# A late chunk's attention in one visit to the matrix engine: x in PSUM banks of its own, and a plan that counts loads and visits

## Chip, cores, metric

One core of one Trainium2 chip. The metric is device time in microseconds (us): the median of the runs shown, lower is better. A profile is one further execution, with every instruction of the engines recorded: PE (TensorE, matmuls), DVE (VectorE), ACT (ScalarE), POOL (GpSimd) and SP, whose queue issues the loads and part of the stores.

## What is computed

A linear attention with a decaying state, and then a two-layer network with a cosine gate on its output.

```python
# r, k, v: (4, 8, 768, 48); w, u: (8, 48)
for t in range(S):
    cur = np.einsum('bhd,bhe->bhde', u[None] * kt, vt)
    y[:, :, t] = np.einsum('bhd,bhde->bhe', rt, state + cur)
    state = w[None, :, :, None] * state + np.einsum('bhd,bhe->bhde', kt, vt)
x = y.transpose(0, 2, 1, 3).reshape(3072, 384)
h = x @ w_in                      # (384, 2048)
out = (h * np.cos(h)) @ w_out     # (2048, 384)
```

## The kernel before

**Attention in chunks.** The 3072 tokens are cut into 24 chunks of 128 tokens; chunk i is tokens of batch i % 4, and its predecessor in the recurrence is chunk i - 4. Within a chunk, the decay is put into k and r (`decT_k`, `decT_r`, `dec_k`), so that attention becomes matmuls: the scores A (k times r), the state update z (k times v), and the output x, which is a part from the state S and a part from v and the masked scores. The first 12 chunks (`EARLY`) go through `early()`, with transposes of k and r on PE (`tr`); the last 12 ("late") go through `in_halves()`: k and r are loaded in a layout that DVE transposes by itself, and the chunk is worked in two halves of 64 tokens. In all chunks POOL does three elementwise operations: r times k, the decay on k, and the product with u.

**The network in steps.** x of three chunks forms a block of 384 tokens; there are 8 blocks, and w_in and w_out are cut into 16 tiles f of 128. One step is one block with one f: on PE nine matmuls of 384 columns (here "H", line 302: 3 contraction tiles times the three products of a high and a low float part), then on ACT and DVE the chain qi, rest, cos, gate, gh, gl, then nine matmuls into the block's accumulator ("O", line 309, three for each chunk). There are 128 steps, so 1152 H and 1152 O matmuls. Blocks 0 to 3 go together through f 0-1, 2-4, 5-9, 10-15; blocks 4 to 7 one after the other. The weight tiles are loaded and converted ("conv": ACT, two DVE operations, POOL, ACT, DVE) while the first blocks run.

**PSUM.** Of the 8 banks, 0-2 hold the accumulators (`B_ACC`), 3-5 H's results (`B_H`), 6-7 the attention of late chunks (`B_ATT`): scores with z, and after them x, take turns in this pair. Early chunks' x use 6-7 or 4-5 (`B_EARLY`).

**Order.** Every piece of work is an operation (`op`) of a planner, with an engine, a due time, an assumed cost and buffers taken from rings. `one_pass` lists the operations in the order in which they can start, earliest due first; after each pass the due times are set to the latest possible starts, for `PASSES` passes; then all is emitted in that order. On each engine the order is fixed from then on. `CHUNK_DUE` and `TILE_SHIFT` are hand-set due times. Up to the first H, PE's planned gaps are filled with dummy matmuls (`warm_up`, one for each 0.2 us of gap).

A late chunk's PE work stands in three operations:

```python
last_A[0] = o_A = zo = op(PE, due - 1.7, 1.12, mm_az, [e_k, e_r, o_kd, l_v], [kT, rT, sp, kb, vb], lat=0.3)
x_1 = op(PE, due - 0.9, 1.1 if c else 0.9, mm_x, [e_r, l_v, e_A, o_s1], [rT, xp, vb, A, S1, *from_0], lat=0.3)
x_t = op(ACT, due - 0.8, 0.2, turn, [x_1], [xp])
xo = op(PE, due - 0.7, 0.6, lambda: from_v(1), [x_t], [xp, vb, A], lat=0.3)
```

`mm_az` is scores (line 1060) and z (line 1076); `mm_x` is x's first part, from the state and from v (line 1123); `from_v(1)` is its rest (line 1123 again), which has to come after a small ACT read, `turn`. Each stands where the planner puts it between H and O.

Of the kernel before, what the change touches and what calls it, by code (L numbers as in the profile page):

```python
# [39 lines left out]
CHUNK_DUE = (-17.2, -100.0, -17.0, -16.6, -14.0, -12.8, -11.2, -10.1, -1.3, 1.2, 13.7, 37.7)  # L40
TILE_SHIFT = (-9.7, 1.9, -82.4, -2.9, -12.4, 2.4, -14.7, 11.2, 1.4, 0.6, 6.8, 16.5)
PASSES = 6
# [20 lines left out]
class Op:  # L63
    def __init__(self, eng, due, cost, lat, emit, after, bufs, behind, port):
        self.eng, self.due, self.cost, self.lat, self.emit = eng, due, cost, lat, emit
        self.after = [o for o in after if o is not None]

        self.behind = behind

        self.port = port  # L70
        self.bufs = bufs
        self.end = None
        self.start = None
        for b in bufs:
            b.users.append(self)


class Plan:
# [9 lines left out]
    def op(self, eng, due, cost, emit, after=(), bufs=(), lat=0.2, line=None, port=False):  # L88

        o = Op(eng, due, cost, lat, emit, after, bufs, self.lines.get(line) if line else None, port)  # L90
# [81 lines left out]
    def one_pass(self):  # L172
# [19 lines left out]
        done, port = [], 0.0  # L192
        while len(done) < len(self.ops):
            best = None
            for eng, ops in cand.items():
                feas = []
                for o in ops:
                    r = self._ready(o)
                    if r is not None:
                        feas.append((max(free[eng], r[0], port if o.port else 0.0), o, r[1]))  # L200
# [3 lines left out]
                pick = min((f for f in feas if f[0] <= t0 + 0.01), key=lambda f: (f[1].due, f[1].seq))  # L204
# [8 lines left out]
            o.gap = t - free[o.eng]  # L213
            o.start, o.end = t, t + o.cost
            free[o.eng] = o.end
            if o.port:
                port = o.end
            cand[o.eng].remove(o)
# [9 lines left out]
def kernel(  # L228
# [47 lines left out]
    F_1 = CUTS[-2]  # L276
# [46 lines left out]
    with ExitStack() as actx:  # L323
# [11 lines left out]
        B_ATT = [pair(6)]  # L335
# [9 lines left out]
        r_all = att.tile([P, 2, H, DP], F32, name="r_all")  # L345
        R_r = [Tile(r_all[:, i]) for i in range(2)]
        raw_r = Tile(r_all.rearrange("q i h d -> q (i h d)")[:, 0 : 2 * DM].bitcast(I32).rearrange("q (f w) -> q f w", w=2))
# [10 lines left out]
        X_r = early_ring("r", 2, [P, H, DP])  # L358
# [10 lines left out]
        R_raw = ring("raw", 2, [P, DM, 2], I32) + [raw_r]  # L369
# [50 lines left out]
        def start_pads():  # L420
            for t in R_k + R_r + R_v + X_k + X_v + X_r:
# [36 lines left out]
        op(PE, -300, 1.6, start_banks, [o_dve], b_0)  # L458
# [22 lines left out]
        o_pow = op(DVE, -90, 3.5, powers, [o_wT, o_dve], [b_w, b_pow])  # L481
# [21 lines left out]
        def tab_copy():  # L503
# [9 lines left out]
            1.2,  # L513
            lambda: nc.sync.dma_start(u_b.rearrange("p h d -> p (h d)"), u.rearrange("h d -> (h d)").partition_broadcast(P)),
            lat=4.6,
# [988 lines left out]
```

## Time and profile before

| | |
|---|---|
| median of 3 runs | 514.6 us (514.23 to 518.33) |
| the profiled execution: its own time | 514.43 us |
| its span, first to last instruction | 512.7 us |
| mean granted TensorE clock | 0.995 |
| PE busy | 498.7 us (97%) |
| DVE, ACT, POOL busy | 383.6, 314.0, 177.3 us |

How to read it: matmuls are pipelined, so that a row's duration (0.34 us for a 384-column matmul) is longer than the distance to the next one (0.17 to 0.18 us); what counts on PE is the distance from start to start. A profile lists each attention matmul on fp32 tiles of an order's row twice (x16 in an order is x32 in the trace). Dummy matmuls count as busy.

### The profile page before, as it was taken

The numbers are of one execution on the slowest core, as the hardware profiler recorded it, in microseconds if no ns is written. First come the engines' busy times: TensorE is split into PE (matmuls) and PEld (weight loads), VectorE is DVE, ScalarE is ACT, GpSimd is POOL, SyncE is SP. The second block draws the span as 40 slices with busy tenths as digits, with TensorE's granted clock in tenths as the row PEclk, the third lists the DMA queues.
The fourth block names the chain that finished last, engine by engine and source line by source line (L and its number), as shares of the span: only waits on it lengthen the run. The fifth ranks groups of instructions, "written<-read, shape, count | busy, mean of one in ns | idle before, by whom it ended". The sixth has DMA issues, their size and how long they took to land.

```text
span 512.7 us, 14821 instructions
## 1 busy us (share of the span) xinstructions
PE 498.7 (97%) x5836; PEld 472.2 (92%) x5836; DVE 383.6 (75%) x788; ACT 314.0 (61%) x805; POOL 177.3 (35%) x183
## 2 busy tenths in 40 slices
PE   7999899999999999999999999999999999999994
PEld 5777789999999999999999999999999999999994
DVE  6888778889899996566777786767767777756452
ACT  1887676777776676547375665574663746654442
POOL 5876512246544463214426224133044042200000
PEclk9999899999999999999999999999999999999999
DMA  9978526577855875426484837448364475110001
GB/s 139 157 152 153 135 79 181 161 161 147 163 138 126 188 144 92 90 40 114 115 173 124 181 93 181 100 130 200 90 169 118 120 178 149 35 49 1 1 1 53
DMA packets 116657, 61.81 MB, mean 121 GB/s; under 512 B 80097, under 2 KB 112482, under 8 KB 116578
## 3 DMA queue, kind: packets, MB, share of 16 engines
q1 hardware_dynamic: 111250, 53.50, 43.0%
q0 software_dynamic: 5184, 7.08, 9.9%
q8 instruction: 47, 0.77, 0.7%
q14 instruction: 32, 0.26, 0.2%
q10 hardware_dynamic: 144, 0.20, 0.1%
HBM read 48.96 MB, written 11.80 MB: 118 GB/s over the span
## 4 chain that ended last, share of the span: by engine, by line
PE 88%; ACT 0%; issue 0%
PE psum L309 40%; PE psum L302 40%; PE psum L1123 4%; PE psum L1060 1%; PE psum L1076 1%; PE psum L989 1%; PE psum L958 0%; PE psum L978 0%; PE psum L1004 0%; PE psum L833 0%; ACT f L1320 0%; PE psum L605 0%
## 5 line engine op out<-in xcount | busy, mean ns | idle before, releaser
L309 PE MATMUL psum<-w_out_hi,gh 128*128 128x384 f32 x384 | 131.9, 344 | 0.0
L302 PE MATMUL psum<-xh,w_in_hi 128*128 128x384 f32 x384 | 131.5, 342 | 0.0
L309 PE MATMUL psum<-w_out_hi,gl 128*128 128x384 f32 x384 | 129.7, 338 | 0.0
L302 PE MATMUL psum<-xh,w_in_lo 128*128 128x384 f32 x384 | 129.7, 338 | 0.0
L309 PE MATMUL psum<-w_out_lo,gh 128*128 128x384 f32 x384 | 129.5, 337 | 0.0
L302 PE MATMUL psum<-xl,w_in_hi 128*128 128x384 f32 x384 | 129.4, 337 | 0.0
L314 ACT ACTIVATE qi<-psum 128x384 int32<-128x384 f32 (+1 forms) x132 | 62.9, 479 | 79.6 <-PE psum L302 78.8
L317 DVE SCALAR_TENSOR_TENSOR f<-psum,qi 128x384 f32<-128x384 f32 (+1 forms) x132 | 71.0, 540 | 47.4 <-ACT qi L314 46.6
L1293 DVE TENSOR_TENSOR gl<-f,gh 128x384 fp32r<-128x384 f32 (+1 forms) x132 | 83.9, 639 | 28.9 <-ACT gh L1290 28.0
L1290 ACT CAST gh<-f 128x384 fp32r<-128x384 f32 (+1 forms) x132 | 65.8, 501 | 40.0 <-DVE f L1287 20.0
L320 ACT ACTIVATE f<-f 128x384 f32<-128x384 f32 (+1 forms) x132 | 67.6, 514 | 30.9 <-DVE f L317 30.4
L1287 DVE TENSOR_TENSOR f<-psum,f 128x384 f32<-128x384 f32 (+1 forms) x132 | 70.6, 537 | 12.8 <-ACT f L320 10.9
L309 PEld LDWEIGHTS psum<-w_out_hi,gh 128*128 128x128 f32 x384 | 72.0, 187 | 2.4 <-issue 0.2
L302 PEld LDWEIGHTS psum<-xh,w_in_hi 128*128 128x128 f32 x384 | 72.5, 189 | 1.6 <-ACT T L942 0.2
L302 PEld LDWEIGHTS psum<-xl,w_in_hi 128*128 128x128 f32 x384 | 72.6, 189 | 0.0
L302 PEld LDWEIGHTS psum<-xh,w_in_lo 128*128 128x128 f32 x384 | 72.6, 189 | 0.0
L309 PEld LDWEIGHTS psum<-w_out_hi,gl 128*128 128x128 f32 x384 | 72.0, 188 | 0.0
L309 PEld LDWEIGHTS psum<-w_out_lo,gh 128*128 128x128 f32 x384 | 72.0, 187 | 0.0
L852 POOL TENSOR_TENSOR T<-T,decT_k 112x512 f32<-112x512 f32 x12 | 17.0, 1414 | 126.7 <-DVE T L847 50.8
L1335 POOL DMA_DIRECT2D out_dram<-f x36 | 33.3, 1080 | 41.0 <-ACT f L1320 40.6
L677 POOL TENSOR_TENSOR f<-f,raw 128x384 int32<-128x384 int32 x23 | 26.2, 1138 | 48.0 <-ACT gh L1290 15.7
L942 ACT ACTIVATE T<-ident,a 128x128 f32<-128x128 f32 x96 | 30.2, 391 | 1.2 <-DVE a L923 1.2
(124 smaller groups left out, 610.8 us busy)
## 6 DMA issues: line engine op xcount, KB each, us to landing
raw<-in_moe_w_out_dram SPq DMA_DIRECT2D x23, 384.0 KB, 3.6
out_dram<-f POOLq DMA_DIRECT2D x36, 192.0 KB, 5.0
raw<-in_moe_w_in_dram SPq DMA_DIRECT2D x72, 64.0 KB, 2.4
out_dram<-f SPq DMA_DIRECT2D x23, 192.0 KB, 2.0
r_all<-in_r_dram SPq DMA_DIRECT2D x40, 96.0 KB, 2.3
raw<-in_moe_w_in_dram SPq DMA_DIRECT2D x10, 384.0 KB, 4.0
raw<-in_k_dram SPq DMA_DIRECT2D x39, 96.0 KB, 2.2
v<-in_v_dram SPq DMA_DIRECT2D x18, 192.0 KB, 4.4
```

The lines of the kernel that those rows point to most:

```text
L302: nc.tensor.matmul(ph, a, b_, start=(i == 0), stop=(i == len(mm) - 1))
L309: nc.tensor.matmul(acc, a[:, ts], b_, start=(first and i == 0), stop=(last and i == 2))
L314: nc.scalar.activation(qi, ph, AF.Copy, scale=INV_2PI, bias=0.25)
L317: nc.vector.scalar_tensor_tensor(q, ph, INV_2PI, qi, op0=ALU.mult, op1=ALU.subtract)
L320: nc.scalar.activation(q, q, AF.Sin, scale=TWO_PI, bias=0.5 * math.pi)
L677: lambda: nc.gpsimd.tensor_tensor(ai(), ai(), cn(), op=ALU.add),
L942: nc.scalar.activation(A[j]()[:, p, :], ident, AF.Copy, scale=ab()[:, h : h + 1])
L1123: nc.tensor.matmul(xv()[G * g : G * g + G, kk, tokens(n)], lhsT, rhs, start=(kk // 2, g) not in opened, stop=True, skip_group_check=True,)
L1287: nc.vector.tensor_tensor(g()[:, cs], ph()[:, cs], q()[:, cs], op=ALU.mult)
L1290: nc.scalar.copy(gh()[:, cs], g()[:, cs])
L1293: nc.vector.tensor_tensor(gl()[:, cs], g()[:, cs], f32(gh())[:, cs], op=ALU.subtract)
L1335: nc.gpsimd.dma_start(dst, ob(), accum_op=ALU.add)
```

## The change

- **Visits.** PE operations carry `moe` (H and O: True; late attention: False) and a late chunk's operations a `visit` number. x's first part and rest of chunk i have visit i, the scores and z of chunk i + 1 have visit i too. When the last operation on an engine has a visit number and another one of that visit could start within `STAY`, the planner takes that one next. x's first part also waits for what the next chunk's scores and z need, and for its own state update.
- **Banks.** A late chunk's x moves from banks 6-7 to 4-5 (`B_X`), which are two of H's three banks; scores with z keep 6-7.
- **The planner's costs.** A change from H or O to late attention costs `SWITCH`; loads and stores have a transfer time (`dma`) on one shared resource, with a landing time worked out from it, and are not planned further than `DMA_AHEAD` ahead of it. Several PE and SP costs are set anew.
- **Due times.** Hand-set shifts for all 24 chunks and all 32 weight tiles in place of those for 12 and 12; 7 passes.
- **Buffers.** `r_all` with its third use as a raw weight buffer goes: early r has a ring of 4, raw weights a ring of 3, early chunks have two more T buffers; `w_out_1` holds 8 tiles in place of 10.
- **Dummies** may stand until the first O, no longer the first H.

```diff
+CHUNK_SHIFT = (
...
+TILE_SHIFT = (
...
+PASSES = 7
+SWITCH, STAY = 0.2, 0.3
+DMA_AHEAD, DMA_FIRST, DMA_LAST, DMA_LAND = 3.0, 1.3, 0.6, 1.95
...
-                        feas.append((max(free[eng], r[0], port if o.port else 0.0), o, r[1]))
+                        t = max(free[eng], r[0], port if o.port else 0.0, moved - DMA_AHEAD if o.dma else 0.0)
+                        feas.append((t, o, r[1]))
...
-                pick = min((f for f in feas if f[0] <= t0 + 0.01), key=lambda f: (f[1].due, f[1].seq))
+                last = on.get(eng)
+                stay = [
+                    f for f in feas if last and last.visit is not None and f[1].visit == last.visit and f[0] <= free[eng] + STAY
+                ]
+                if stay:
+                    pick = min(stay, key=lambda f: (f[0], f[1].due, f[1].seq))
+                else:
+                    pick = min((f for f in feas if f[0] <= t0 + 0.01), key=lambda f: (f[1].due, f[1].seq))
...
+            if o.moe is False and last and last.moe:
+                o.end += SWITCH
+            on[o.eng] = o
...
+            if o.dma:
+                moved = max(moved, t + DMA_FIRST) + o.dma
+                o.lat = max(moved + DMA_LAST - o.end, DMA_LAND)
...
-    F_1 = CUTS[-2]
+    F_1 = NF // 2
...
-        B_ATT = [pair(6)]
+        B_ATT, B_X = [pair(6)], [pair(4)]
...
-        X_r = early_ring("r", 2, [P, H, DP])
+        X_r, X_T = early_ring("r", 4, [P, H, DP]), early_ring("T", 2, [P, NP, C])
...
-        R_raw = ring("raw", 2, [P, DM, 2], I32) + [raw_r]
+        R_raw = ring("raw", 3, [P, DM, 2], I32)
...
-            bk = B_EARLY if i < EARLY else B_ATT
+            bk = B_EARLY if i < EARLY else B_X
...
-                A, sp, S1 = Buf(R_T), Buf(bk), Buf(R_s)
+                A, sp, S1 = Buf(R_T), Buf(B_ATT), Buf(R_s)
...
-                last_A[0] = o_A = zo = op(
-                    PE, due - 1.7, 1.12, mm_az, [e_k, e_r, o_kd, l_v], [kT, rT, sp, kb, vb], lat=0.3
-                )
+                ready = [e_k, e_r, o_kd, l_v]
+                last_A[0] = o_A = zo = op(PE, due - 1.7, 0.88, mm_az, ready, [kT, rT, sp, kb, vb], lat=0.3)
+                zo.visit, zo.moe = i - 1, False
+                if i - 1 in visits:
+                    visits[i - 1].after += ready
...
-                    1.1 if c else 0.9,
+                    0.99,
                     mm_x,
-                    [e_r, l_v, e_A, o_s1],
+                    [e_r, l_v, e_A, o_s1, *o_s2],
...
+                x_1.visit, x_1.moe = i, False
+                visits[i] = x_1
                 x_t = op(ACT, due - 0.8, 0.2, turn, [x_1], [xp])
-                xo = op(PE, due - 0.7, 0.6, lambda: from_v(1), [x_t], [xp, vb, A], lat=0.3)
+                xo = op(PE, due - 0.7, 0.27, lambda: from_v(1), [x_t], [xp, vb, A], lat=0.3)
+                xo.visit, xo.moe = i, False
...
             if i < EARLY:
-                due = CHUNK_DUE[i]
+                due = -1.5 * (EARLY - i) - 1.0
...
+            due += CHUNK_SHIFT[i]
...
-            if s == 0:
-                o_first = oh
+            oh.moe = True
...
+                oo.moe = True
+                if s == 0 and t == 0:
+                    o_first = oo
```

What this does to the order, at three places. In the rows a name's number is the buffer's; lines are those of each kernel, and H is line 302 before and 328 now, O 309 and 335, x 1123 and 1160, scores 1060 and 1093, z 1076 and 1109.

**PE, a late chunk.** Before, chunk 14's x with two O groups between its parts; its scores and z (buffers T_102, v_83) stand 36 rows ahead of it, alone, between an O and an H:

```order
L1123 MATMUL psum<-T_102,s_109 32x64 x16
L1123 MATMUL psum<-T_102,s_105 32x64 x16
L1123 MATMUL psum<-T_103,v_83 32x64 x16
L309 MATMUL psum<-w_out_hi_2188,gh_124 128x384
L309 MATMUL psum<-w_out_hi_2188,gl_126 128x384
L309 MATMUL psum<-w_out_lo_2189,gh_124 128x384
L309 MATMUL psum<-w_out_hi_2188,gh_124 128x384
L309 MATMUL psum<-w_out_hi_2188,gl_126 128x384
L309 MATMUL psum<-w_out_lo_2189,gh_124 128x384
L1123 MATMUL psum<-T_103,v_83 32x64 x16
```

Now, chunk 13's x with the scores and z of chunk 14 between its parts, an O before and after:

```order
L335 MATMUL psum<-w_out_lo_1918,gh_127 128x384
L1160 MATMUL psum<-T_105,s_111 32x64 x16
L1160 MATMUL psum<-T_105,s_108 32x64 x16
L1160 MATMUL psum<-T_106,v_81 32x64 x16
L1093 MATMUL psum<-T_107,T_101 64x64 x16
L1109 MATMUL psum<-v_82,k_79 48x48 x16
L1160 MATMUL psum<-T_106,v_81 32x64 x16
L335 MATMUL psum<-w_out_hi_1917,gh_127 128x384
```

Three visits have become one here. Over the whole order, late attention's groups between H or O number 36 before (three for each of 12 chunks) and 22 now: six are of this full form, two join a chunk's scores and z to the x of the chunk before, the rest stand as before.

**SP, the loads of early chunks 7 to 11.** Before, from the r of chunk 7 on, two loads of w_in tiles (raw_127, raw_128; the order of the loads is also that of the transfers) stand before the k of chunk 10:

```order
L763 DMA early_r_96<-in_r_dram 128x4x48 x2
L540 DMA raw_127<-in_moe_w_in_dram 32x2x256 x4
L540 DMA raw_127<-in_moe_w_in_dram 64x256 x2
L755 DMA early_v_94<-in_v_dram 128x8x48
L755 DMA v_81<-in_v_dram 128x8x48
L763 DMA k_80<-in_k_dram 128x4x48 x2
L763 DMA r_all<-in_r_dram 128x4x48 x2
L763 DMA early_k_89<-in_k_dram 128x4x48 x2
L763 DMA r_all<-in_r_dram 128x4x48 x2
L755 DMA v_82<-in_v_dram 128x8x48
L540 DMA raw_128<-in_moe_w_in_dram 32x2x256 x4
L540 DMA raw_128<-in_moe_w_in_dram 64x256 x2
```

Now, from the k of chunk 9 on, one w_in tile stands before the k of chunk 10 (early_k_89), and k and r of chunk 11 come before the next:

```order
L796 DMA early_k_88<-in_k_dram 128x4x48 x2
L796 DMA early_r_96<-in_r_dram 128x4x48 x2
L788 DMA v_82<-in_v_dram 128x8x48
L565 DMA raw_130<-in_moe_w_in_dram 32x2x256 x4
L565 DMA raw_130<-in_moe_w_in_dram 64x256 x2
L796 DMA early_k_89<-in_k_dram 128x4x48 x2
L796 DMA early_k_90<-in_k_dram 128x4x48 x2
L796 DMA early_r_97<-in_r_dram 128x4x48 x2
L788 DMA early_v_91<-in_v_dram 128x8x48
L565 DMA raw_131<-in_moe_w_in_dram 32x2x256 x4
L565 DMA raw_131<-in_moe_w_in_dram 64x256 x2
```

The second w_in tile has moved behind the last k and r, and the first from behind chunk 7's r to behind chunk 8's v.

**PE, the end of the early part.** Before, one H stands between chunks' transposes long before this place; here come chunk 8's z (line 1004), chunk 9's scores (958), chunk 11's transposes (833), chunk 10's scores, and two H in a row of which the first matmul is shown, with three chunks' x and z and chunk 11's scores still to come behind them:

```order
L1004 MATMUL psum<-v_83,k_80 48x48 x8
L958 MATMUL psum<-T_103,T_97 128x128 x8
L833 MATMUL psum<-ident,early_k_91 112x64 x8
L833 MATMUL psum<-ident,early_r_96 112x64 x8
L958 MATMUL psum<-T_99,T_101 128x128 x8
L302 MATMUL psum<-xh,w_in_hi 128x384
```

Now chunk 11's transposes (866) are followed by chunk 9's x (1011, 1022), chunk 10's scores (991), chunk 9's z (1037) and the very first H:

```order
L866 MATMUL psum<-ident,early_k_90 112x64 x8
L866 MATMUL psum<-ident,early_r_97 112x64 x8
L1011 MATMUL psum<-T_101,s_113 32x128 x16
L1022 MATMUL psum<-early_T_98,early_v_91 32x128 x4
L1022 MATMUL psum<-T_104,early_v_91 32x128 x4
L1022 MATMUL psum<-early_T_98,early_v_91 32x128 x4
L1022 MATMUL psum<-T_104,early_v_91 32x128 x4
L991 MATMUL psum<-T_102,T_103 128x128 x8
L1037 MATMUL psum<-early_v_91,early_k_88 48x48 x8
L328 MATMUL psum<-xh,w_in_hi 128x384
```

The H have moved behind the early chunks; behind the first H remain chunk 11's scores and two chunks' x and z. On POOL the three operations of all 12 chunks now stand before any weight tile's addition; before, two such additions stood among them.

More of the change, by code (lines that the diff above doesn't have):

```diff
@@ L63, with __init__ @@
 class Op:
-    def __init__(self, eng, due, cost, lat, emit, after, bufs, behind, port):
-        self.eng, self.due, self.cost, self.lat, self.emit = eng, due, cost, lat, emit
+    def __init__(self, eng, due, cost, lat, emit, after, bufs, behind, port, dma):
+        self.eng, self.due, self.cost, self.lat, self.emit = eng, round(due, 3), cost, lat, emit
+        self.dma = dma
         self.after = [o for o in after if o is not None]
@@ L70, in __init__ @@
         self.port = port
+        self.visit = None
+        self.moe = None
         self.bufs = bufs
@@ L86, in __init__, with op @@
         self.lines = {}
-    def op(self, eng, due, cost, emit, after=(), bufs=(), lat=0.2, line=None, port=False):
-        o = Op(eng, due, cost, lat, emit, after, bufs, self.lines.get(line) if line else None, port)
+    def op(self, eng, due, cost, emit, after=(), bufs=(), lat=0.2, line=None, port=False, dma=0.0, behind=None):
+        o = Op(eng, due, cost, lat, emit, after, bufs, self.lines.get(line) if line else behind, port, dma)
         if line:
@@ L213, in one_pass @@
             o.gap = t - free[o.eng]
+            last = on.get(o.eng)
             o.start, o.end = t, t + o.cost
+            if o.moe is False and last and last.moe:
+                o.end += SWITCH
+            on[o.eng] = o
             free[o.eng] = o.end
@@ L512 @@
             -23.9,
-            1.2,
+            0.5,
             lambda: nc.sync.dma_start(u_b.rearrange("p h d -> p (h d)"), u.rearrange("h d -> (h d)").partition_broadcast(P)),
-            lat=4.6,
+            lat=2.0,
+            dma=0.6,
+            behind=o_w,
         )
@@ L639, in cn @@
                 return raw()[:, :, 0]
-            o0 = op(SP, due - 3.5, 1.6 if part else 3.2, lambda: load_raw(i, raw, True), [behind], [raw], lat=3.4)
+            o0 = op(
+                SP,
+                due - 3.5,
+                0.5 if part else 3.8,
+                lambda: load_raw(i, raw, True),
+                [behind],
+                [raw],
+                dma=1.4 if part else 1.5,
+            )
             o2 = op(
@@ L718 @@
         last_A = [None]
-        early_done = []
-        r_first = Buf([raw_r])
+        early_done, visits = [], {}
         last_z = [None] * B
@@ L748, in chunk @@
             trp = Buf(B_TR)
-            kT, rT = Buf(R_T), Buf(R_T)
+            R_Tc = R_T + X_T if i < EARLY else R_T
+            kT, rT = Buf(R_Tc), Buf(R_Tc)
             xp = Buf(bk)
@@ L782, in chunk @@
                 ks, rs = Buf(R_raw), Buf(R_raw)
-            rbs = [rb] if late else [rb, r_first]
+            rbs = [rb]
             def load_r():
@@ L881, in chunk @@
                     due - 2.5,
-                    0.55,
+                    0.59,
                     tr,
-                    [l_r, l_k if first else o_kd, o_pool, o_pads],
+                    [l_r, l_k if first else o_kd, o_pool, o_pads, o_wT],
                     [*rbs, kb, trp, rT, kT],
@@ L934, in early @@
             def early():
-                A = [Buf(R_T) for _ in range(2)]
+                A = [Buf(R_Tc) for _ in range(2)]
                 Ap = [Buf(B_ONE) for _ in range(2)]
@@ L1339 @@
                         s + 2.5,
[L1340 removed]
+                        0.45 if f0 == 0 else 1.1,
                         st,
@@ L1343 @@
                         [ob],
-                        lat=2.5,
+                        dma=0.6 if f0 == 0 else 1.0,
                     )
```

42 lines of the change are left out of this document (22 added, 20 removed).

## The prediction

> **What bounds the kernel now.** First the page's busy times, then the busy time by stretches, then PE's rows.
>
> ```profile
> PE 498.7 (97%) x5836; PEld 472.2 (92%) x5836; DVE 383.6 (75%) x788; ACT 314.0 (61%) x805; POOL 177.3 (35%) x183
> ```
>
> 97% is an average that counts dummy matmuls. By stretches (length, then busy time and instructions of PE, PEld, DVE, ACT, POOL, granted clock, DMA share, GB/s):
>
> ```profile
> 20.00:25.00 5.00, 5.00 (x125) 4.25 (x125) 4.44 (x10) 4.93 (x16) 3.89 (x4) 1.00 0.89 161
> 55.00:60.00 5.00, 3.86 (x38) 3.64 (x39) 4.37 (x8) 4.47 (x14) 2.37 (x3) 0.73 0.65 169
> 83.00:219.00 136.00, 136.00 (x781) 136.00 (x780) 117.48 (x223) 93.38 (x210) 58.86 (x59) 1.00 0.65 143
> 219.00:481.00 262.00, 261.87 (x3530) 249.71 (x3529) 185.56 (x378) 150.68 (x403) 72.05 (x66) 1.00 0.47 115
> ```
>
> From 83 to 481 us PE is idle for 0.13 us of 398: there the time is the sum of what PE executes, and only fewer or denser matmuls help. Before that, as from 20 to 25 us, PE, DVE, ACT and POOL are all nearly full and the loads run at 161 GB/s; there the time is set by when the early chunks get through. The chain that ended last prices the network's work (start, length, matmuls):
>
> ```profile
> 58.05 4.56 PE psum L302 x18
> ...
> 93.17 1.56 PE psum L302 x9
> 94.73 1.58 PE psum L309 x9
> 99.45 3.12 PE psum L302 x18
> ```
>
> 128 steps of 1.56 + 1.58 make 402 us, and the change leaves them alone. So I sum two terms: what late attention costs PE, and what PE does outside H and O up to the end of early attention.
>
> **Term 1: visits.** PE's rows of chunk 12: scores and z, the O around x's first part, x's rest (start, time to the end of the row, what):
>
> ```profile
> 220.15 0.34 PE L309 MATMUL psum<-w_out_lo,gh 128*128 128x384 f32 x1
> 220.42 0.69 PE L1060 MATMUL psum<-T,T 48*64 48x64 f32 x32
> 220.93 0.54 PE L1076 MATMUL psum<-v,k 64*48 64x48 f32 x32
> 221.40 0.45 PE L309 MATMUL psum<-w_out_hi,gh 128*128 128x384 f32 x1
> 221.69 0.34 PE L309 MATMUL psum<-w_out_hi,gl 128*128 128x384 f32 x1
> ...
> 224.48 0.34 PE L309 MATMUL psum<-w_out_lo,gh 128*128 128x384 f32 x1
> ...
> 226.13 0.34 PE L309 MATMUL psum<-w_out_hi,gl 128*128 128x384 f32 x1
> ...
> 227.87 0.34 PE L302 MATMUL psum<-xh,w_in_lo 128*128 128x384 f32 x1
> 228.14 0.45 PE L1123 MATMUL psum<-T,v 64*32 64x64 f32 x32
> 228.52 0.44 PE L309 MATMUL psum<-w_out_hi,gh 128*128 128x384 f32 x1
> 228.81 0.33 PE L309 MATMUL psum<-w_out_hi,gl 128*128 128x384 f32 x1
> ```
>
> The pitch inside O is 1.58 / 9 = 0.176. From the last O to the first score it is 0.27, so entering costs 0.09 to 0.10; from the first O behind to the second 0.29, so leaving costs 0.11: about 0.205 a visit, and the rows around x's rest say the same. (From O's end to where the next O would have stood, the three visits displace 1.19, 1.30 and 0.59, together 3.08.) The order has 22 visits for 36: 14 joins. If a join cost nothing, 14 x 0.205 = **2.9 us** would go; that is one end. The other is that a join costs as much as leaving and entering: 0. No row shows x next to scores, but early attention has other tile shapes side by side in one visit:
>
> ```profile
> 71.05 0.34 PE L309 MATMUL psum<-w_out_lo,gh 128*128 128x384 f32 x1
> 71.32 1.16 PE L958 MATMUL psum<-T,T 48*128 48x128 f32 x16
> 72.41 0.67 PE L978 MATMUL psum<-T,s 48*32 48x128 f32 x32
> 73.01 1.08 PE L989 MATMUL psum<-T,early_v 128*32 128x128 f32 x32
> 74.02 0.44 PE L309 MATMUL psum<-w_out_hi,gh 128*128 128x384 f32 x1
> 74.30 0.34 PE L309 MATMUL psum<-w_out_hi,gl 128*128 128x384 f32 x1
> ```
>
> The last of 16 scores starts near 71.32 + 1.16 - 0.28 = 72.20 (0.28 is taken as one matmul's length), and x's first 0.21 later, against a pitch of 0.06 within the scores: 0.15 for the change of shape. In chunk 12, z's last starts near 220.93 + 0.54 - 0.21 = 221.26 (0.21 taken likewise) and O 0.14 later, against a pitch of 0.015: 0.12 of that sort is in the visit's own length already. A join so costs some 0.03 more than nothing: 14 x (0.205 - 0.03) = **2.4 us**, which I take, as the nearest rows have it.
>
> The Trainium skill, "TensorEngine Tiling (Array Packing)", section Key Properties, says that a change of tiling mode drains the engine. By it, a full visit still changes mode four times (in, x to scores, z to x, out) for six in three visits, and with a change at half of 0.205 the term would be some 1.4 (an estimate from that page's rule). The 0.15 above agrees that a change inside a visit is not free; the time by the rule, 508.9, lies in the forecast's band.
>
> What else the visits touch is priced at nothing, with this cover: x's ACT read and its copies run beside H and O; the added wait (x also waits for the next chunk's operands) has a whole chunk's distance, some 20 us, of loads ahead of it; behind a waiting x on PE stands everything, so a late one is paid in full.
>
> **Term 2: the early part.** Before, rows around the first H, chunk 11's transposes and chunk 9's z:
>
> ```profile
> 42.25 0.44 PE L302 MATMUL psum<-xh,w_in_hi 128*128 128x384 f32 x1
> ...
> 56.14 0.44 PE L833 MATMUL psum<-ident,early_k 64*112 64x64 f32 x8 [1.55 <-POOL early_k L874]
> 56.64 1.42 PE L958 MATMUL psum<-T,T 48*128 48x128 f32 x16
> 57.98 0.69 PE L302 MATMUL psum<-xh,w_in_hi 128*128 128x384 f32 x1
> ...
> 65.64 0.34 PE L302 MATMUL psum<-xh,w_in_lo 128*128 128x384 f32 x1
> 65.91 0.56 PE L1004 MATMUL psum<-early_v,early_k 128*48 128x48 f32 x16
> 66.41 0.44 PE L302 MATMUL psum<-xh,w_in_hi 128*128 128x384 f32 x1
> 66.69 0.34 PE L302 MATMUL psum<-xl,w_in_hi 128*128 128x384 f32 x1
> ```
>
> A visit of z displaces 66.69 - 65.64 - 2 x 0.174 = 0.70; scores with x 74.30 - 71.05 - 2 x 0.176 = 2.90; x alone 2.90 - 1.09 (71.32 to 72.41) = 1.81. Behind 57.98, early attention still needs 2.90 + 2 x 1.81 + 3 x 0.70 = 8.6, and the 18 H there take 4.56 for 3.12 at a clock of 0.73: 1.4 lost, of which 0.1 is the entry. One H (1.56) is done already. So H and O could start unbroken at 57.98 + 8.6 + 1.3 - 1.6 = **66.3**.
>
> In the new order the first H stands behind chunk 11's transposes (0.50, 56.14 to 56.64), chunk 9's x (1.61, 72.41 to 74.02), scores (1.09) and z (0.50): 3.7 in all. Behind it remain 2.90 + 1.81 + 2 x 0.70 = 6.1. What decides is when chunk 11's k is ready, which POOL's rows show:
>
> ```profile
> 11.89 1.09 POOL L864 TENSOR_TENSOR f<-early_r,k 128x384 f32<-128x384 f32 x1 [1.40 <-DMA early_r<-in_r_dram]
> ...
> 48.63 1.02 POOL L864 TENSOR_TENSOR f<-early_r,early_k 128x384 f32<-128x384 f32 x1 [3.47 <-DMA early_r<-in_r_dram]
> ...
> 55.07 1.01 POOL L874 TENSOR_TENSOR early_k<-early_k,dec_k 128x384 f32<-128x384 f32 x1
> ```
>
> At 11.89 it had waited for chunk 2's r, the 6th load of 192 KB, at 48.63 for chunk 10's r, the 34th when a w_in tile counts as two: 36.74 / 28 = 1.31 us each. In the new order chunk 10's k is the 33rd (one tile ahead of it in place of two) and lands at 11.89 + 27 x 1.31 = 47.3; chunk 11's r, the 35th, at 49.9. POOL then does five operations of 1.02 up to chunk 11's decayed k (product, decay, u for chunk 10; product, decay for chunk 11): 52.4. So PE's transposes start at 52.4, in place of 56.14, and the first H at 56.1. H and O could start unbroken at 56.1 + 6.1 = 62.2: a gain of **4.1 us**, which I take: between these loads stands a w_in tile, as between those of before. The other pace is the 161 GB/s of 20 to 25 us, 1.22 a load: k at 44.8, POOL done at 49.9. PE itself has some six and a half chunks of 3.7 to do after 25 us, to 49, and chunk 10's transposes and two z (1.5) stand ahead of chunk 11's, so 51 is its own bound: a first H at 54.7 and a gain of 5.5. The w_in tile's own conversion ends on POOL two operations after chunk 11's k (54.4), on ACT and DVE 1.1 later: 55.5, just in time. Weight tiles for O load later than before by one w_in tile, 2.6 us, and are needed 11.7 behind the first H (four H, two x, scores and z): hidden. The buffers' new rings and `w_out_1`'s size I price at nothing, since loads there start on the queue's turn, not on a buffer.
>
> **Sum.** 514.43 - 4.1 - 2.4 = 507.9 for the profiled execution; it stands 0.2 below the median of the runs, so **508.0**.
>
> **Rivals.**
>
> - *The clock drops again.* Chunk 10's decayed k is ready at 49.4 by the same count; with its transposes and two z PE is done at 51 and waits 1.4 for chunk 11's. Before, a wait of 1.55 stood ahead of the 0.73. Price 1.3, and a late w_in tile would add to it: 509.2 to 510.5. The page "TensorE: Matmul & The Clock Gate" of the Trainium skill, section "What's actually happening", has the clock fall after an idle window of about 3.4 us, so that such a wait alone would not do it; the trace, which had it after 1.55, disagrees, and the rival stays.
> - *Joins save nothing* (the visits do not do what they are for): 510.3.
> - *H runs out of banks.* x needs banks 4 and 5 at once, and until its copies are out, H has bank 3 alone. At the end of the kernel, a step's bank was free 2.3 us after H:
>
> ```profile
> 485.61 0.49 ACT L314 ACTIVATE qi<-psum 128x384 int32<-128x384 f32 x1 [0.31 <-PE psum L302]
> ...
> 487.29 0.56 DVE L1287 TENSOR_TENSOR f<-psum,f 128x384 f32<-128x384 f32 x1 [0.59 <-ACT f L320]
> ```
>
>   The gate ends at 487.85, qi began at 485.61. Between such a step's operations DVE also has late chunks' transposes:
>
> ```profile
> 248.97 1.09 DVE L847 STREAM_TRANSPOSE T<-r_all 128x512 f32<-128x512 f32 x1
> ```
>
>   In the new order most x have two or more groups between the youngest H but one and themselves, 3.7 us or more; the youngest has 2.1 if four O stand between. Where the youngest sits in bank 4 or 5, x waits 0.2 to 0.5: 12 x 0.3 = 3.6 and 511.5. It becomes **slower** if a DVE transpose of 1.09 stands ahead of the gate in each of the 12: 12 x (0.3 + 1.09) = 16.7, and 524.7; it decides from the point where the youngest H is closer than 2.3 us to x's banks. Against it: DVE is 71% busy there, and PE hardly waited in 398 us with the same chain.
> - *Loads at the fast pace*: 506.5.
>
> **How the numbers follow.** A measurement of this kernel tells about 1% (5.1 us) from no change: faster is below 509.4, slower above 519.7. Forecast, 506.8 to 509.4: 0.46. Fast loads or more, 504.5 to 506.8: 0.12. Clock or a late first H, 509.2 to 511: 0.16, a quarter of it below 509.4. Joins for nothing: 0.09. Banks, light: 0.12; banks, heavy: 0.05. Faster 0.46 + 0.12 + 0.04 = 0.62; slower 0.05; the same 0.33. The range, 504.5 to 512.5, leaves out the heavy case, part of the light one, and gains beyond both ends of the terms.
>
> **What the new profile would show.** Chunk 11's transposes near 52 and the first H near 56, with clock 1.00 from 55 to 60; H and O unbroken from about the point where 6 us of attention are behind the first H; 22 late visits, a full one displacing about 2.7 (3.08 for three before: 1.19, 1.30, 0.59) and a gap of some 0.15 between x and scores; no PE wait behind 83. Wrong would be: PE waiting for DVE's gate or x's copies in front of an x or an H (banks), a wait for POOL or a DMA at a visit (the added dependence), the first H behind 58 (loads), or full visits above 3.

## The result, and the profile after

The changed kernel takes 520.64 us (median of 17 runs, 517.28 to 522.43) against 514.57 for the kernel before on the same chip: 1.0107 times as long, 95% interval 1.0084 to 1.0130. It is slower by about 1.1%; forecast were 508.0 and a range of 504.5 to 512.5. The profiled execution took 521.12, with a span of 519.4.

The busy times by stretches, in the columns of the rows before (length, then busy time and instructions of PE, PEld, DVE, ACT, POOL, granted clock, DMA share, GB/s):

```profile
20.00:25.00 5.00, 5.00 (x128) 4.16 (x128) 4.62 (x10) 4.93 (x16) 4.67 (x6) 1.00 1.04 171
45.00:50.00 5.00, 3.19 (x31) 2.62 (x33) 4.16 (x9) 3.76 (x12) 3.32 (x4) 0.50 1.01 177
50.00:55.00 5.00, 5.00 (x74) 3.67 (x74) 3.24 (x6) 2.52 (x8) 2.60 (x3) 0.50 0.46 118
55.00:60.00 5.00, 5.00 (x131) 3.84 (x125) 1.63 (x4) 2.17 (x6) 1.02 (x1) 0.66 0.71 158
83.00:219.00 136.00, 135.47 (x976) 133.54 (x974) 121.38 (x232) 93.00 (x218) 62.13 (x61) 1.00 0.70 155
219.00:481.00 262.00, 259.46 (x3322) 251.96 (x3321) 181.76 (x372) 153.37 (x399) 69.19 (x64) 0.99 0.46 112
```

Two things differ from before. From 45 to 60 us TensorE runs at about half its clock, and "busy" hides it: PE is 5.00 of 5.00 busy, with 74 matmuls where the first stretch shows 128. And from 219 to 481 PE is idle for 2.54 us, where it had been idle for 0.13.

PE's matmuls date the loss. The 301st matmul of H and O starts at 118.65 before and at 123.41 after: **4.8 us** are lost by then. From there to the start of the last one go 387.0 before and 389.4 after, **2.4** more; from that to the end of the execution 8.8 and 8.3. Together that is the 6.7 between the profiled executions.

**The early 4.8.** Rows of DVE, ACT and PE of the changed kernel (start, length, what; in brackets the idle time ahead and what ended it):

```profile
44.67 0.36 DVE L687 TENSOR_SCALAR f<-raw 128x384 int32<-128x384 int32 x1 [4.10 <-DMA raw<-in_moe_w_in_dram]
44.94 0.55 DVE L956 TENSOR_REDUCE a<-f 128x8 f32<-128x384 f32 x1
45.41 0.68 DVE L925 TENSOR_TENSOR T<-psum,decT_r 112x512 f32<-112x512 f32 x1
...
46.12 0.59 ACT L945 COPY T<-psum 112x512 f32<-112x512 f32 x1 [4.07 <-DVE T L925]
...
46.81 0.68 PE L866 MATMUL psum<-ident,early_k 64*112 64x64 f32 x8 [3.63 <-issue]
```

DVE takes its instructions in order: the row sum and L925 run right behind L687, in the order of its queue. The first operation on `w_in` tile 0 (L687) stands ahead of chunk 9's row sum (L956) and chunk 8's decayed r (L925), and waits 4.10 for the tile's load. Behind L925 comes ACT's copy, which frees the transposes' bank, and only then PE goes on, after 3.63. "issue" there means that PE's own record names no releaser; ACT's row, ending at 46.71, does. The clock is 0.50 from 44.8 to 58.4. The chain of waits has the first H at 64.77, where 56.1 was predicted:

```profile
64.77 1.76 PE psum L328 x9
```

The loads and POOL were not late. POOL had chunk 11's decayed k ready at 51.72 (predicted 52.4), but PE came to chunk 11's transposes only 9.2 later (POOL's row, and PE's in the chain):

```profile
50.70 1.02 POOL L907 TENSOR_TENSOR early_k<-early_k,dec_k 128x384 f32<-128x384 f32 x1
...
60.90 0.66 PE psum L866 x16
```

**The late 2.4.** One joined visit has a hole in it, a stop of PE that no other engine ends (PE's rows), and behind it the clock is 0.50 for 3.4 us (stretches of 2 us):

```profile
354.42 0.53 PE L1109 MATMUL psum<-v,k 64*48 64x48 f32 x28
357.49 0.29 PE L1109 MATMUL psum<-v,k 64*48 64x48 f32 x4 [2.54 <-issue]
```

```profile
358.00:360.00 2.00, 2.00 (x32) 1.91 (x9) 1.97 (x5) 0.48 (x1) 0.00 (x0) 0.70 0.62 189
360.00:362.00 2.00, 2.00 (x8) 2.00 (x7) 0.78 (x3) 0.51 (x1) 0.00 (x0) 0.50 0.00 0
```

PE stops after 28 of z's 32 matmuls, whose operands are all there, for 2.54. Here nothing in the trace releases it: no semaphore, no other engine. The half clock behind costs 1.7 more. Around 146, PE also waits for `w_out`'s high half and a gate, some 0.9 by the starts of its matmuls.

A joined visit without a hole is as short as meant to be, by the O in front of and behind it:

```profile
263.98 0.34 PE L335 MATMUL psum<-w_out_lo,gh 128*128 128x384 f32 x1
...
266.71 0.44 PE L335 MATMUL psum<-w_out_hi,gh 128*128 128x384 f32 x1
266.99 0.34 PE L335 MATMUL psum<-w_out_hi,gl 128*128 128x384 f32 x1
```

266.99 - 263.98 - 2 x 0.1745 = 2.66, where the three visits displaced 3.08: 0.21 a join, or 2.9 for the 14 if all are like this one. So the late part adds up: -2.9 + 2.5 + 1.7 + 0.9 = 2.2 of the 2.4.

### The profile page after: what moved, and what is told of

Same layout as the page of the kernel before. It is cut to its first block, busy times and chain, and to the rows that moved or that the text cites. A ratio compares the mean times of both kernels' runs of the same rounds, so it can differ in the third digit from the quotient of the medians.

```text
span 519.4 us, 14841 instructions
## 1 busy us (share of the span) xinstructions
PE 501.1 (96%) x5840; PEld 476.5 (92%) x5840; DVE 383.7 (74%) x788; ACT 315.4 (61%) x805; POOL 177.2 (34%) x183
## 4 chain that ended last, share of the span: by engine, by line
PE 88%; DVE 4%; issue 3%; DMA 2%; SPq 1%; ACT 1%; POOL 0%; DVEq 0%; ACTq 0%
PE psum L335 37%; PE psum L328 36%; PE psum L1160 3%; PE psum L991 2%; PE psum L1022 2%; PE psum L1093 1%; SPq L565 1%; DMA out_dram<-f 1%; PE psum L1037 1%; PE psum L866 1%; PE psum L1011 1%; PE psum L1395 1%; DVE gl L1334 1%; PE psum L1109 1%; DMA raw<-in_moe_w_out_dram 1%
## 5 line engine op out<-in xcount | busy, mean ns | idle before, releaser
L328 PE MATMUL psum<-xh,w_in_hi 128*128 128x384 f32 x384 | 130.1, 339 | 0.0
L1334 DVE TENSOR_TENSOR gl<-f,gh 128x384 fp32r<-128x384 f32 (+1 forms) x132 | 80.7, 616 | 23.2 <-ACT gh L1331 22.6
L710 POOL TENSOR_TENSOR f<-f,raw 128x384 int32<-128x384 int32 x32 | 37.8, 1215 | 68.5 <-DVE f L699 25.1
L1379 POOL DMA_DIRECT2D out_dram<-f x36 | 32.0, 1033 | 50.1 <-ACT f L1364 33.5
L950 POOL TENSOR_TENSOR f<-f,u_b 128x384 f32<-128x384 f32 x24 | 27.0, 1127 | 0.2
```

What stands on the lines that cost most here:

```text
L328: nc.tensor.matmul(ph, a, b_, start=(i == 0), stop=(i == len(mm) - 1))
L710: lambda: nc.gpsimd.tensor_tensor(ai(), ai(), cn(), op=ALU.add),
L950: e1, due - 2.2, c1, lambda: n1.tensor_tensor(heads(mb), heads(mb), u_b, op=ALU.mult), [o_m, o_u], [mb], port=True
L1334: nc.vector.tensor_tensor(gl()[:, cs], g()[:, cs], f32(gh())[:, cs], op=ALU.subtract)
L1379: nc.gpsimd.dma_start(dst, ob(), accum_op=ALU.add)
```

## Experiments on the early part

All runs below, but for one control, move instructions in the queues of the changed kernel or add dummy matmuls, and leave its arithmetic alone. Diffs show an engine's queue, or the line of code. Ratios are to the kernel before, on the same chip, with 95% intervals. The runs stand on several chips, so two of them are best compared by their ratios. A profile is one execution, and its time lay up to 3 us from the median of its run.

**One DVE instruction moved.**

```diff
 L1224 TENSOR_TENSOR xl<-psum,xh
-L687 TENSOR_SCALAR f<-raw            (w_in tile 0)
 L956 TENSOR_REDUCE a<-f              (chunk 9)
 L925 TENSOR_TENSOR T<-psum,decT_r    (chunk 8)
...
 L996 COPY_PREDICATED T<-upper,psum
+L687 TENSOR_SCALAR f<-raw
 L699 SCALAR_TENSOR_TENSOR f<-raw,f
```

> One DVE instruction of the changed kernel moves 13 places back: the first operation on w_in tile 0 (L687) stands directly ahead of the second (L699), behind chunk work in place of ahead of it. All loads and PE's order stay. Theory A (DVE's queue held up by the tile's load, then half clock): the wait of 3.63 at 46.81 goes, PE reaches chunk 10's transposes near 49 and chunk 11's near 51.7 as POOL lets it, the clock stays near 1.00 from 45 to 59, the first H comes near 56 for 64.77, and the time falls by 8.8 from 520.6 to some 512 (ratio to before 0.995). Rival B (chunk 10's k, landed at 46.6 behind the same load, sets the pace anyway): first H past 61, time above 517. Rival C (the visits of late chunks are what costs): no more than 2 us change.

Measured: 518.20, ratio 1.0060 (1.0029 to 1.0091). The wait stayed, under another name:

```profile
44.66 0.55 DVE L956 TENSOR_REDUCE a<-f 128x8 f32<-128x384 f32 x1 [3.43 <-POOL f L950]
```

Chunk 9's row sum, next in the queue, now waited for POOL to 44.66, and L925 behind it again. Clock 0.50 for 10.2 us, first H at 63.77. Theory A was too simple: two instructions stood in the way, one behind the other. The time missed its 512 by 6.

**The load behind the chunks' loads.** SP's queue, on top of the run above:

```diff
-L565 DMA raw<-in_moe_w_in_dram       (w_in tile 0, 6 issues)
 L796 DMA early_k<-in_k_dram          (chunks 10 and 11)
 L796 DMA early_r<-in_r_dram          (chunk 11)
+L565 DMA raw<-in_moe_w_in_dram
```

> As the run with the moved DVE instruction, and on SP's queue w_in tile 0's load (4.93 us of issue) moves behind chunk 10's and 11's k and chunk 11's r. These land some 4.9 earlier, k of chunk 10 near 42, so POOL no longer waits and PE alone sets the pace: chunk 11's transposes near 50.5, the first H near 54.5 if the tile's conversion is done by then (it lands near 48). Expected 1.5 below the run with the moved instruction alone, about 510.5. Rival: the tile now ends last, PE waits for its low half in front of H, and the first H stays at 56 or later: no gain, or up to 2 slower than that run.

Measured: 517.58, ratio 1.0070 (1.0037 to 1.0102), the same as without it. The loads did land earlier: POOL began on chunk 10 at 44.33, for 47.75 in the run above. But DVE's row sum still stood ahead of L925 and PE's transposes still came at 46.28: with that queue unmended, earlier loads buy nothing.

**The wait filled with work.** 32 dummies into a free bank, while everything else stays:

```diff
+                o is trs[9] and warm_up(32)
                 o.emit()
```

> The changed kernel with 32 dummy matmuls (128 x 256, into a bank not in use) ahead of chunk 9's transposes, where PE waited 3.63: the wait stays, but PE executes in it. Nothing else moves. If the half clock from 45 to 59 comes from that wait: the clock stays near 1.00, the 11.7 us that PE worked at 0.50 from 47 to 58.7 shrink to about 6, the first H comes near 59, and the time falls by 5.9 to 514.7. If something else holds PE there (POOL, loads) or lowers the clock: no more than 2 us.

Measured: 524.13, ratio 1.0183 (1.0144 to 1.0222). The early half came out as expected; stretches of that run, and its first H in the chain of waits:

```profile
45.00:50.00 5.00, 4.57 (x63) 3.58 (x61) 4.44 (x9) 4.11 (x13) 3.71 (x4) 1.00 0.90 180
50.00:55.00 5.00, 5.00 (x181) 3.95 (x179) 4.34 (x10) 4.16 (x13) 3.28 (x4) 1.00 0.38 104
```

```profile
59.41 1.76 PE psum L328 x9
```

The wait still ended at 46.58, but the clock stayed at 1.00: 181 matmuls from 50 to 55 for 74, the first H 5.4 earlier. So of the 8.7 by which the first H missed my number, 5.4 are the half clock that the wait brought in the changed kernel's profile, and the other 3.3 are about the wait itself. The 5.4 are not fixed: two runs further below have the same early queues. With all visits apart, PE waited 4.23, was at 0.50 for 3.4 only and had its first H at 61.76; with one visit apart, it waited 3.75, was at 0.50 for 10.2 and had it at 63.90. With the shortest half clock the early part is 1.8 behind the kernel before, in place of 4.8, and in none of the three is it ahead.

And yet the run with the filled wait is slower than the changed kernel. PE stopped four times behind 83 where it had stopped once. That contradiction decided what to look at next.

## Experiments on the holes in PE

The DMA view lists queues by kind. One kind had escaped me; whole execution of the changed kernel (packets, MB, share):

```profile
q1 hardware_dynamic: 111250, 53.50, 43.3%
q0 software_dynamic: 5184, 7.08, 9.8%
q8 instruction: 47, 0.77, 0.6%
```

The queues carry instructions too: 47 packets of 16.4 KB. PE's records hold 2 x 5840 weight loads and matmuls and 57 others, 11,737 in all: about 250 to a packet. In the hole, from 354 to 356, there is one:

```profile
q1 hardware_dynamic: 1873, 0.41, 121.1%
q8 instruction: 1, 0.02, 3.5%
```

By its own times it started at 354.87 and ended at 355.98, and PE went on 1.5 later. The transfers' queue is busy around it; whether that delayed the piece is taken up in the last section. Numbering PE's instructions from 0 in the order of their start, it stopped ahead of number 8385 = 32 x 256 + 193.

That gives **theory D**: PE's instructions arrive in pieces of 256. By the earliest packets, a piece is asked for some 294 instructions ahead of its first. In H and O these are 147 matmuls, 25 us; a joined visit has 192 matmuls, 384 instructions in 2.5 us, so the last 294 ahead of a boundary can go by in 1.9. If the piece takes longer, PE runs dry. Before, the O and H between the three visits kept every 294 at 4.9 us or more.

**Visits apart again.** The 14 joins undone by one group each:

```diff
 L1160 MATMUL x, first part
+L335 MATMUL psum<-w_out_hi,gh        (one O of 3, from behind)
 L1093 MATMUL scores
 L1109 MATMUL z
+L335 MATMUL psum<-w_out_hi,gh        (the next O)
 L1160 MATMUL x's rest
-L335 MATMUL psum<-w_out_hi,gh
-L335 MATMUL psum<-w_out_hi,gh
```

> The changed kernel with its 22 late visits broken into 36 again: behind each of 14 joins one O (3 matmuls) or H group that stood after the visit is moved between its pieces. Early part, banks and loads stay. Term 1 (a join saves 0.175): slower by 2.4 than the changed kernel, about 523. Rival (long runs of small matmuls make PE's instruction stream run dry, as in the 2.54 at 357.49): that stall goes, late clock back to 1.00, and the time is the same or up to 3 lower, 517.5 to 521.

Measured: 521.21, ratio 1.0121 (1.0083 to 1.0159), not to be told from the changed kernel: neither the 2.4 nor the other theory came out in the time. The hole stayed, at the same instruction, 2.1 long: an O of 0.53 between the pieces raises the time for the 294 from 1.9 to 2.6, too little. The profile bears out term 1 all the same. From the 301st matmul of H and O to the last it takes 389.3, which is 387.2 without the hole (no half clock came behind it). That is the 387.0 of the kernel before, which has 36 groups too; the run further below with 24 groups and no hole takes 384.4.

**The same early part with three counts of instructions.** The filled wait above has 32 matmuls more ahead of the late part than the changed kernel. With 16 wide dummies there, and 32 early ones joined to 16, the count is the old one:

```diff
+                o is trs[9] and wide(16, 4)   # 128 x 512 each
                 o.emit()
```

> As the run with the filled wait, but PE's count of instructions is the changed kernel's: 16 dummies of 128 x 512 in the wait, and 32 of the early 128 x 256 dummies joined to 16 of 128 x 512. Theory D (PE's instructions come in pieces of 256; where a boundary falls into a joined visit PE runs dry, so the stalls hang on how many instructions stand ahead): the first H near 59.4, the stalls as in the changed kernel, one of 2.5 near 349 in z and none of the other three, so 521.1 - 5.4 = 515.7. Rival (stalls come by chance or with the early timing): three or four stalls as in the run before, 522 to 524.

Measured: 517.81, ratio 1.0047 (1.0018 to 1.0077). And with 60 narrow ones, 60 more:

```diff
+                o is trs[9] and wide(60, 1)   # 128 x 128 each
                 o.emit()
```

> As the run with the filled wait, but with 60 dummies of 128 x 128 in place of 32 of 128 x 256: about the same time in the wait, 56 instructions more. Theory D, from the changed kernel's times of PE's instructions with every boundary moved by 120 and the fetch taking some 4.1 us from request to use: seven stalls (in the visits near 217 light, then 231, 266, 301, 331, 397 of 2 us each and 429 of 1), 10 to 12 us in all, and half clock behind some of them: 527 to 531. Rival (chance): one to four stalls, 519 to 525.

Measured: 532.61, ratio 1.0313 (1.0272 to 1.0353). PE's waits behind 83 with no releaser, in the runs with the old count, 32 more and 60 more (total, times, longest):

```profile
PE psum L1109 <- issue: 2.9, 1, 2.9
```

```profile
PE psum L1160 <- issue: 6.3, 3, 2.7
PE psum L335 <- issue: 1.1, 1, 1.1
```

```profile
PE psum L1109 <- issue: 6.4, 3, 3.0
PE psum L1160 <- issue: 4.7, 4, 2.4
```

One hole, four, and the seven forecast, 11.1 us of the 10 to 12; the time is 1.6 above the forecast's upper end. The late work and its order are the same in all three; only where the boundaries fall in it differs, and 15 us hang on that. The run with the old count missed its 515.7 by 2: in its profile the first tile's conversion came late (first H at 62.13 for 59.41), and the half clock at its hole lasted 6.8 for 3.4.

**Before, with 60 more.** The control:

```diff
+            for _ in range(2 * h):    # 128 x 128, in place of the first 60
             for _ in range(n):        # 128 x 256, the others
```

> The kernel before with 60 of its early dummies of 128 x 256 made into 120 of 128 x 128: 60 matmuls more ahead of everything, in about the same time. Theory D: before's late visits, three to a chunk with O and H between, never use up 299 of PE's instructions in less than 4.9 us, so no boundary can make a stall: PE waits under 0.3 us behind 83 and the time is that of before within 1 us. Rival (the count of instructions costs by itself, or any kernel of this size has such stalls): 3 us or more slower.

Measured: 514.37, ratio 0.9990 (0.9962 to 1.0017). The list of PE's waits from 83 to 500 is empty, as in the kernel before. The count costs nothing by itself; it takes the joined visits.

**Only the visit with the hole taken apart**, all else as changed:

```diff
 L328 MATMUL psum<-xh,w_in_lo
+L1093 MATMUL scores
+L1109 MATMUL z
 L335 MATMUL psum<-w_out_hi,gh        (6 O and one H)
...
 L1160 MATMUL x, first part
-L1093 MATMUL scores
-L1109 MATMUL z
-L1160 MATMUL x's rest
 L335 MATMUL psum<-w_out_hi,gh        (4 O)
+L1160 MATMUL x's rest
```

> The changed kernel, only the late visit in which PE stalled taken apart (scores and z 6 O and one H earlier, x's rest 4 O groups later). Early part as in the changed kernel, with its wait and half clock. Theory D: no stall behind 83, late half clock gone, 3.5 to 4 less than the changed kernel's 520.64: 516.6 to 517.1, ratio to before 1.004. Rival (the visit hardly matters): 519 or more.

Measured: 517.08, ratio 1.0043 (1.0021 to 1.0065), as forecast: 3.6 less than the changed kernel, or 3.3 by the two ratios. PE's waits from 83 to 500 are then a gate and a weight, and the stretch of the hole is full:

```profile
219.00:481.00 262.00, 262.00 (x3344) 254.24 (x3322) 183.37 (x376) 154.57 (x402) 68.87 (x64) 1.00 0.45 111
```

PE's numbered instructions give this:

| kernel | matmuls ahead | holes behind 83 | shortest times for 294 instructions (us) |
|---|---|---|---|
| before; with 60 more | 0; +60 | 0; 0 | 4.9; 4.8 |
| changed | 0 | 1 | 1.9, then 4.3 |
| joins undone by an O | 0 | 1 | 2.6, then 5.0 |
| filled, old count | 0 | 1 | 1.9, then 4.3 |
| filled, 32 more | +32 | 4 | 1.9, 2.0, 2.0, 2.3 |
| filled, 60 more | +60 | 7 | 1.8 to 3.9 |
| that visit apart | 0 | 0 | 4.3 |

All 17 holes of these and the other runs stand at a number 256 n + 193. From the 294th instruction ahead to PE's going on, these pieces took 3.6 to 5.1 us, and PE went on 1.25 to 1.57 behind the packet's end. Every boundary with 3.9 us or less had a hole, none with 4.3 or more.

## Experiments towards a better version

**Both DVE instructions moved**, and then the visit with the hole apart as well.

```diff
-L687 TENSOR_SCALAR f<-raw            (to ahead of L699)
-L956 TENSOR_REDUCE a<-f              (chunk 9)
 L925 TENSOR_TENSOR T<-psum,decT_r    (chunk 8)
 L1059 TENSOR_TENSOR psum<-psum,s
 L1060 TENSOR_TENSOR s<-psum,pq
 L1224 TENSOR_TENSOR xl<-psum,xh
 L996 COPY_PREDICATED T<-upper,psum
+L956 TENSOR_REDUCE a<-f
```

> The changed kernel with two DVE instructions moved back: the first operation on w_in tile 0 to ahead of the second, and chunk 9's row sum (L956, which stood in the way at 44.66 when only the first was moved) behind chunk 8's decayed r, state, xl and mask. Theory A, now with two waits in DVE's queue: PE's transposes of chunk 9 come near 43.5 for 46.5, the clock stays at 1.00, first H near 56 to 57, time 512.4 with the stall of 2.5 near 348 still there. Rival: k of chunk 10 and POOL's chain behind it hold PE (transposes of chunk 10 past 50, of chunk 11 past 54): first H 59 or later, 515 or more.

> As the run with both DVE instructions moved, and the one late visit in which PE stalled is taken apart: scores and z stand 6 O and one H earlier, x's rest 4 O groups later. All other visits stay joined. Theory D: no stall of PE behind 83, late clock 1.00, 4 us less than that run (2.5 of the stall, 1.6 of half clock behind it, less 0.2 for a visit more): 508.4 if that run is at 512.4. Rival: the stall moves to the next joined visit and the time stays.

Measured: 518.92, ratio 1.0074 (1.0048 to 1.0100), and 515.41, ratio 0.9999 (0.9978 to 1.0020). The 3.5 between them, where 4 were expected, go with the hole: PE has none behind 83 in the second run. The first run was forecast at 512.4, though. The early forecast failed again: chunk 9's transposes came at 43.2 and PE was busy all the time from 45 to 50 at full clock, and then stood for 5.3 (ACT and PE rows of the second run; 5.5 in the first):

```profile
54.33 0.56 ACT L679 ACTIVATE raw<-raw 128x384 int32<-128x384 uint32 x1 [6.35 <-DMA raw<-in_moe_w_in_dram]
54.78 0.46 ACT L1219 CAST xh<-psum 128x384 fp32r<-128x384 f32 x1
...
55.89 1.52 PE L1037 MATMUL psum<-v,k 128*48 128x48 f32 x32 [5.34 <-DVE xl L1224]
```

The same fault, one tile on and on another engine: ACT's first operation on the second `w_in` tile waits 6.35 for its load, with x's high half behind it, for which DVE's low half and then PE's z wait.

**These queues put right too.**

```diff
 ACT:
-L679 ACTIVATE raw<-raw               (second tile)
 L1219 CAST xh<-psum
...
 L720 CAST w_in_hi<-f                 (first tile)
+L679 ACTIVATE raw<-raw
 DVE:
+L687, L699 on the first tile         (ahead of chunk 10's row sum)
 L956 TENSOR_REDUCE a<-f              (chunk 10)
...
-L956 TENSOR_REDUCE a<-f              (chunk 11)
 L925 TENSOR_TENSOR T<-psum,decT_r    (chunk 10)
+L956 TENSOR_REDUCE a<-f
...
+L687 on the second, third tile       (each next to its L699)
 SP:
 L788 DMA early_v<-in_v_dram          (chunks 10 and 11)
+L565 DMA raw<-in_moe_w_in_dram       (third tile, from ahead of them)
```

> As the run with both DVE instructions moved and one visit apart, and the next waits behind w_in tiles taken out of the queues too: on ACT the second tile's first operation (L679, which waited 6.35 to 54.33 with chunk work behind it) goes behind the first tile's high half; on DVE the second and third tile's first operation go next to their second one, the first tile's two go ahead of chunk 10's row sum, and chunk 11's row sum goes behind chunk 10's decayed r; on SP the third tile's load goes behind v of chunks 10 and 11. Theory A (every one of these waits is a first operation on a tile standing ahead of chunk work in an engine's queue): no wait of PE over 1 us from 44 to 60, clock near 1.00, chunk 11's transposes near 52.5, first H near 56.5 for 62.85, time 509 for 515.4, below before (ratio 0.988). Rival: POOL's chain or the tile itself now ends last: first H 59 or later, 512 or more.

Measured: 511.07, **ratio 0.9924 (0.9899 to 0.9950)**: 0.8% better than the kernel before, 2 us behind its forecast. The stretches that had been at half clock, and the late ones:

```profile
45.00:50.00 5.00, 5.00 (x152) 3.67 (x148) 3.46 (x7) 3.32 (x11) 1.87 (x2) 1.00 0.86 161
50.00:55.00 5.00, 2.26 (x64) 1.81 (x64) 2.39 (x5) 2.23 (x6) 4.50 (x6) 1.00 0.58 135
55.00:60.00 5.00, 3.91 (x108) 2.94 (x103) 4.09 (x10) 4.10 (x13) 0.86 (x1) 1.00 0.73 182
83.00:219.00 136.00, 135.98 (x1010) 134.31 (x1009) 120.83 (x231) 91.88 (x216) 65.06 (x63) 1.00 0.71 156
219.00:481.00 262.00, 262.00 (x3315) 254.33 (x3315) 181.60 (x373) 154.17 (x401) 65.25 (x61) 1.00 0.44 108
```

The clock holds, and no PE wait is left behind 83. But from 50 to 60 PE is idle for 3.8: a wait of 2.0 for DVE's xl, and four of 0.3 to 0.6. The 2.0 are the old fault once more: chunk 10's row sum waits 2.95 on DVE for POOL, to 51.44, with the mask and xl behind it, although x's high half, from which xl is made, was done at 48.95. The first H is at 60.08, and its chain of waits goes back to chunk 11's r, which lands at 51.7. By PE's matmuls this run is level with before at the 301st of H and O (118.71 for 118.65), 2.6 shorter from there to the last, and 0.7 shorter behind it. The 2.6 agree with its 12 joins (12 x 0.205 = 2.5); where the 0.7 come from is not shown. **So the lead over before is made in the late part, most of it by the visits, and the new early plan, mended this far, gains nothing.**

**The first tile's load behind those of chunks 10 and 11**, and its first operations on ACT and DVE further back:

```diff
 SP:
-L565 DMA raw<-in_moe_w_in_dram       (first tile)
 L796 DMA early_k, early_r            (chunks 10 and 11)
+L565 DMA raw<-in_moe_w_in_dram
```

> As the run with the queues put right and one visit apart (511.07), and on SP the first w_in tile's load goes behind chunk 10's and 11's k and chunk 11's r, its first operations on ACT and DVE behind the chunk work up to chunk 10's copies. If the landing of these loads now sets the early part (chunk 11's r landed at 51.7 there and POOL's product for chunk 11 started at 51.83): POOL ends chunk 11's k near 51 for 53.9, chunk 11's transposes come near 52.8 for 54.66, first H near 58 for 60.08, time 509. Rival: the tile's own conversion (landing near 50, then 5 operations of 3.5 in all) takes its place, first H 59.5 or later, no gain beyond 0.5.

Measured: 511.54, ratio 0.9945 (0.9923 to 0.9967): no gain. The first H came at 58.83 for 60.08. But just ahead of it PE had waited 0.9 and 1.3 for DVE and ACT work that now stands behind the first tile's operations, and the H itself ran at half clock:

```profile
58.83 2.96 PE psum L328 x9
```

So both the rival and half of the theory are true: the wait moved to the tile, and the clock took back the 1.2 that was gained.

## Why the prediction was wrong, step by step

- **What bounds the kernel**: right. Behind 83 the time is the sum of what PE executes, and early on it is when the chunks get through.
- **Term 1, 2.4 us from 14 joins**: right in kind and near in size. The full visit shown displaces 2.66 (predicted 2.7), so a join saves 0.21 there (0.175 taken, 0.205 the upper end). The value worked from the drain rule of the Trainium skill, "TensorEngine Tiling (Array Packing)", section Key Properties, was 1.4; the trace has 2.9 by that visit, and 2.8 lie between the late parts of the runs with 36 and 24 groups. So the changes of shape inside a visit cost nothing measurable beyond what the separate visits had paid.
- **"No PE wait behind 83"**: wrong. I counted what a visit takes of PE's time and not what it takes of PE's instruction stream; the number of matmuls stays, but not how densely they come. None of my rivals had this mechanism: it cost 2.5 and 1.7 of half clock here, more than the joins gave, and 11 of holes alone at another count. Shown by the runs with 32 and 60 more, the control and the visit apart.
- **Term 2, "the first H at 56.1, a gain of 4.1"**: the step that failed most, by 8.7 us. It went from loads to POOL to PE. The first half came out (chunk 11's decayed k at 51.72 for 52.4); the step "PE's transposes start at 52.4", with PE's own work done by 51, did not: they started at 60.90. It left out the engines between: the line that the w_in tile's conversion ends just in time was about the tile, while the tile's first operations stand in DVE's and ACT's queues ahead of chunk work. Their waits were 4.10 on DVE and, once that was mended, 6.35 on ACT. The load of a tile takes 4.93 on SP and landed 7.1 behind the start of its issue, and I never asked who queues behind its first reader.
- **The clock**: the rival "the clock drops again" named the right thing at a price of 1.3. A wait of 3.63, where before had 1.55, brought 13.6 us at 0.50 in the profile (10.2 and 3.4 in two others of the same early queues), where before had 3.4; filling the wait gave back 5.4.
- **H running out of banks, and joins saving nothing**: did not happen. No PE wait for a gate or a copy exceeds 0.3 behind 83 in the changed kernel.
- Still open: why chunk 11's r lands at 51.7 in the mended run and not at the 49.9 of my pace, and what a plan with the true landing times would give early; that was not tried. So the gain of 4.1 was not reached by any run, and that the queues alone kept it away is not shown.

## What to carry to other kernels

Before packing small matmuls densely on PE, count how long the last 294 instructions ahead of each boundary of its stream (every 256 here) take, against the time of a piece (3.6 to 5.1 us here), and take a dense stretch apart where that is too short. In an in-order queue, put the first operation on a loaded tile next to its second one, behind work that is ready: a transfer that lands a few us late otherwise stops the engines downstream, and PE's clock can add to the loss. When a "busy" engine falls behind, compare its instruction counts per stretch with the granted clock.

## What the runs showed of the hardware

- PE's instructions are fetched in pieces of 256 (16.4 KB) over a DMA queue of their own. That the kernel's transfers delay them is not shown: behind 83 us, over all runs, a piece's packet took 1.0 us in the median of the 227 that met a DMA share of other queues below 0.1 (at most 1.45), and 1.1 in the median of the 48 that met a share of 1.0 to 1.3 (at most 2.40). The Trainium skill, "Runtime: NRT & Kernel Launch", section "Instruction fetch mechanics", states the pieces of 16 KiB and 256 instructions and says that crossing a boundary is mostly hidden. The sizes agree; hidden it was in the kernel before and in H and O, while the 17 holes of these runs are up to 3.0 us long. I had not weighed that section in the prediction.
- TensorE's clock: of 20 waits of PE between 1.3 and 3.0 us, 14 were followed by half clock within 3 us, or ended in it, and so were all six of over 3 us. At late holes it lasted 3.4 us, in one run 6.8; early it lasted 3.4 to 13.6, and every length was one to four times 3.41. The Trainium skill's page "TensorE: Matmul & The Clock Gate", section "What's actually happening", has free-running windows of about 3.4 us. The lengths agree, and so does the missing sharp limit: a wait of 1.33 was enough in one run, one of 2.69 was not in another.
- 60 more harmless matmuls in the early part moved the end by 15 us in one order of the late work and by less than 1 in the other.
